# Weight words put together in PSUM banks, the root's scratch in a bank, and the value product on 128 rows, in an attention and mixture kernel

## The chip, the cores and the metric

The kernel runs on one core of a Trainium2 chip. The time is the device time of the whole program in microseconds (us); runs are compared by their median. A core has five engines that work side by side, each through its own list of instructions in a fixed order: TensorE (PE in the profile; its weight loads are PEld), VectorE (DVE), ScalarE (ACT), GpSimd (POOL) and SyncE (SP, which here only issues transfers). SBUF is the working memory. PSUM has eight banks of 128 rows by 512 four-byte words; TensorE writes its products there, and VectorE and ScalarE read and write it in this kernel.

## The reference

Attention over 8 batches, 12 heads, 448 positions and head width 64, with the queries and keys normalised by their root mean square, and behind it a channel-mixing layer of width 768 with 1024 hidden units. Weights come as 8-byte floats.

```python
def rmsnorm(x, g):
    rms = np.sqrt(np.mean(x * x, axis=-1, keepdims=True) + 1e-06)
    return x / rms * g
q_n, k_n = (rmsnorm(q, g_q), rmsnorm(k, g_k))
scores = 1.0 / np.sqrt(64) * np.matmul(q_n, k_n.transpose(0, 1, 3, 2))
attn = softmax(scores)                       # exp(scores - max) / (sum + 1e-09)
x = matmul(attn, v), heads side by side      # (8, 448, 768)

x_prev = x moved down by one position, zeros first
xk = mu_k * x + (1.0 - mu_k) * x_prev
xr = mu_r * x + (1.0 - mu_r) * x_prev
k = np.maximum(xk @ w_k, 0.0)
v = k * k @ w_v
r = 1.0 / (1.0 + np.exp(-(xr @ w_r)))
return r * v
```

## The kernel before, in words

Products run on 16-bit halves: each operand is split into a high part and a low part ("hi", "lo"), and three of the four products are summed in a bank.

Three streams of work are written out and interleaved. A small planner in the kernel's last loop always lets the stream with the smallest clock write its next piece (rates such as `ATT_STEPS` and `W_RATE2`); behind it a scheduler orders each engine's instructions by its own model of their times. The order that the chip runs is fixed by that, and it is shown below for the places that matter.

*Attention.* The 48 pairs of heads go one after the other; two pairs make a quad. `load` fetches keys and queries of a quad. `prep` normalises them: ScalarE squares (L166), GpSimd folds the squares (L167) and multiplies the keys with the gains (L169), VectorE sums (L170), scales (L172, L173) and takes the reciprocal root in `rsqrt` (L67 to L72, a guess from the bits and three Newton rounds, on 128x28 numbers); GpSimd multiplies by it (L179), ScalarE takes the high part (L184), GpSimd the low part (L186, "nat"), and transfers on SyncE's queue turn them into the stacks "stk". `vprep` finds a power of two to scale each pair's values: ScalarE squares and sums (L203), a tiny matmul spreads the sums (L204) into the bank "tr", VectorE takes the maximum (L206), and the values are split (L211, L215). `group_scores` multiplies for two tiles of 128 rows at a time (the last group has one) into a bank for each tile, VectorE takes the maximum (L258), ScalarE the exponential (L259). `group_probs` scales by the sum (L271, L272) into high (ScalarE, L277) and low (VectorE, L278), and a transfer transposes them to "pT". `attend` makes the value product in the bank "av": eleven passes for each head, of which the one on the low part of slot 3 uses 64 rows and the others 128; ScalarE reads it out (L303).

*Weights.* `weight_tile` builds 20 tiles of 128 columns: eight of w_k, six of w_r, six of w_v. Each is loaded in two chunks of 384 (w_k, w_r) or 512 (w_v) numbers a row, so 28 and 12 chunks. The two halves of an 8-byte float are put together to a 4-byte one: ScalarE scales the upper half's magnitude (L403), VectorE shifts (L404), ors in bits of the lower half (L405) and the sign (L406). Then a Gram product in "av" (L412), its diagonal (L416), a sum over rows (L417) and a maximum (L418) give the tile's scale, and the tile is split into 16-bit halves (on GpSimd and ScalarE for tiles 1 to 13, L423 to L425, else L427 and L428).

*The mixing layer.* `moe` takes each batch when its six pairs are done: `mix` (L367 to L376), then `prod` (L456) with the key weights (xk, wk), the gate weights (xr, wr) and the output weights (kk, wv), each into one of two banks "mm".

The eight banks before: "sc" four and "mm" two, "av" one, "tr" one. In the first six pairs (`PRO`) every third score tile lies in an "mm" bank.

```python
tag, nb = ("mm", MM_BUFS) if i < PRO and (i * NT + t0 + j) % 3 == 2 else ("sc", 4)
banks.append(ps.tile([P, 512], F32, name=tag, bufs=nb))
```

Of the kernel before, what the change touches and what calls it, by code (L numbers as in the profile page):

```python
# [7 lines left out]
F32 = mybir.dt.float32  # L8
F16 = mybir.dt.float16
BF16 = mybir.dt.bfloat16  # L10
I32 = mybir.dt.int32
AF = mybir.ActivationFunctionType
ALU = mybir.AluOpType
# [15 lines left out]
PRO = 6  # L29
# [34 lines left out]
def rsqrt(nc, pool, y, a, n, tag):  # L64
    t = pool.tile([P, n], F32, name=tag)
    yi = y.bitcast(I32)
    nc.vector.tensor_scalar(out=yi, in0=a.bitcast(I32), scalar1=1, scalar2=None, op0=ALU.logical_shift_right)  # L67
    nc.vector.tensor_scalar(out=yi, in0=yi, scalar1=-1.0, scalar2=float(0x5F3759DF), op0=ALU.mult, op1=ALU.add)
    for _ in range(NEWTON):
        nc.vector.tensor_tensor(out=t, in0=y, in1=y, op=ALU.mult)  # L70
        nc.vector.scalar_tensor_tensor(out=t, in0=t, scalar=-0.5, in1=a, op0=ALU.mult, op1=ALU.mult)
        nc.vector.scalar_tensor_tensor(out=y, in0=t, scalar=1.5, in1=y, op0=ALU.add, op1=ALU.mult)  # L72


def attn_moe_kernel(tc, q, k, v, g_q, g_k, mu_k, mu_r, w_k, w_v, w_r, out):
# [14 lines left out]

    def allmax(src, n, r):
        pt = ps.tile([P, 512], F32, name="tr", bufs=1)
# [21 lines left out]
    rsqrt(nc, small, gm[:, 1:2], gm[:, 0:1], 1, "rs1")  # L114
# [46 lines left out]
    def prep(u):  # L161
        ss = small.tile([P, 2 * NSS], F32, name="ss", bufs=2)
# [11 lines left out]
        rsqrt(nc, small, ss[:, NSS:2 * NSS], ss[:, 0:NSS], NSS, "rs28")  # L174
        yield
        T = [ap_.tile([P, 2, 2 * NT, HD], F16, name="stk", bufs=3) for x in range(2)]
        for n, t in enumerate(LD.pop(u)):
            tv = t.rearrange("p h (t d) -> p (h t) d", d=HD)
            nc.gpsimd.tensor_tensor(out=tv, in0=tv, in1=spread(ss[:, NSS + 2 * NT * n:NSS + 2 * NT * (n + 1)], HD), op=ALU.mult)  # L179
# [13 lines left out]
    def vprep(i):  # L193
# [8 lines left out]
        pt = ps.tile([P, 512], F32, name="tr", bufs=1)  # L202
# [34 lines left out]
    def group_scores(i, t0, n):  # L237
# [5 lines left out]
        for j in range(n):  # L243
            tag, nb = ("mm", MM_BUFS) if i < PRO and (i * NT + t0 + j) % 3 == 2 else ("sc", 4)
            banks.append(ps.tile([P, 512], F32, name=tag, bufs=nb))
# [41 lines left out]
    PASSES = [(hl, c, P) for c in range(3) for hl in range(2)] + [(0, 3, P), (1, 3, HD)] + [(0, c, P) for c in range(4, 7)]  # L287
# [104 lines left out]
    def weight_tile(nm, w, kt, c, ci):  # L392
# [4 lines left out]
        for i in range(0, kt, hk):  # L397
# [5 lines left out]
            nc.scalar.activation(out=f[:, i:i + hk, :], in_=top.bitcast(F32), func=AF.Abs, scale=F64_EXP)  # L403
            nc.vector.tensor_scalar(out=fb, in0=fb, scalar1=3, scalar2=None, op0=ALU.logical_shift_left)  # L404
            nc.vector.scalar_tensor_tensor(out=fb, in0=low, scalar=29, in1=fb, op0=ALU.logical_shift_right, op1=ALU.bitwise_or)  # L405
# [204 lines left out]
```

## Time and profile before

| what | value |
|---|---|
| median of 3 runs | 1267.06 us (1266.27 to 1267.16) |
| profiled execution | 1263.01 us |
| its span, first to last instruction | 1261.2 us |
| mean granted TensorE clock | 0.911 |
| TensorE busy | 1017.4 us (81%) |
| VectorE busy | 901.4 us (71%) |
| ScalarE busy | 794.4 us (63%) |
| GpSimd busy | 681.4 us (54%) |

Busy time is the sum over a whole run of stages that differ. In rows of groups, "L405 DVE ... wf<-raw,wf 128x384 ... x28 | 23.1, 835 | 0.1" reads: line 405, VectorE, writes tile wf from raw and wf, 28 instructions, 23.1 us in all, 835 ns each, and 0.1 us of idle time of that engine just before them. In rows of single lines three durations stand as minimum/median/maximum. In rows of waits stand the total, the number of times and the longest, in us. The rows of stages give for each engine its busy us in the stretch, then the granted TensorE clock, the DMA engines' busy share and GB/s.

### The profile page before, as it was taken

Reading aid. Unit: us, or ns where it says so; the run is one execution under the profiler, and the core shown is the slowest. Engines: PE = TensorE matmul, PEld = TensorE weight load, DVE = VectorE, ACT = ScalarE, POOL = GpSimd, SP = SyncE. Lnnn points to the kernel's source line nnn. Section 1 sums busy time; section 2 is a strip of 40 time slices with the busy share of each in tenths; the row PEclk is TensorE's granted clock in tenths of the full one; section 3 lists DMA queues with packets and bytes.
Section 4 is the critical chain, followed back from the end, with each engine's and each line's share of the span. In section 5 each row is a group of like instructions: output and inputs, shape, how many; then the busy total and the mean of one; then the engine's idle time right before and its main releaser. Section 6 shows DMA issues by size and latency. Waiting matters only on the chain. (4 is left out here: it accounts for less than half of the span.)

```text
span 1261.2 us, 18897 instructions
## 1 busy us (share of the span) xinstructions
PE 1017.4 (81%) x5935; PEld 471.4 (37%) x5935; DVE 901.4 (71%) x2356; ACT 794.4 (63%) x1756; POOL 681.4 (54%) x678
## 2 busy tenths in 40 slices
PE   1125545586799999889999899898989999999998
PEld 0002222233244344433443444344434444344454
DVE  5886899979967868675786667776887687667200
ACT  3266656566756777577676765776778676876311
POOL 2642465736655657375467536674568455523731
PEclk9956656588799999998999999999989999999999
DMA  7589977978586878768777676978986787776101
GB/s 161 119 152 168 178 155 160 172 153 165 110 148 134 146 145 167 139 131 142 143 147 147 128 138 138 167 132 152 167 162 129 151 150 125 136 144 102 26 13 38
DMA packets 456356, 172.77 MB, mean 137 GB/s; under 512 B 411200, under 2 KB 452672, under 8 KB 456256
## 3 DMA queue, kind: packets, MB, share of 16 engines
q1 hardware_dynamic: 423328, 132.24, 59.2%
q10 hardware_dynamic: 32928, 39.34, 12.8%
q8 instruction: 46, 0.75, 0.2%
q14 instruction: 54, 0.44, 0.1%
HBM read 61.41 MB, written 11.01 MB: 57 GB/s over the span
## 5 line engine op out<-in xcount | busy, mean ns | idle before, releaser
L278 DVE SCALAR_TENSOR_TENSOR ph<-sc,sums,ph 128x448 f16<-128x448 f32 x322 | 210.0, 676 | 87.8 <-ACT ph L277 87.2
L259 ACT ACTIVATE sc<-sc,sums 128x448 f32<-128x448 f32 x322 | 193.3, 612 | 108.8 <-DVE sums L258 91.5
L235 PE MATMUL sc<-stk 64*128 64x448 f16 (+1 forms) x1104 | 189.9, 379 | 68.1 <-DVE ph L278 49.7
L456 PE MATMUL mm<-wvh,kk 128*128 128x384 f16 x896 | 234.6, 330 | 0.1
L456 PE MATMUL mm<-xk,wkh 128*128 128x448 f16 x768 | 220.9, 366 | 12.7 <-ACT kf L478 6.0
L277 ACT ACTIVATE ph<-sc,sums 128x448 f16<-128x448 f32 x322 | 189.6, 645 | 50.3 <-DMA pT<-ph 15.7
L258 DVE TENSOR_REDUCE sums<-sc 128x1 f32<-128x448 f32 x322 | 187.8, 613 | 22.8 <-PE sc L235 22.3
L456 PE MATMUL mm<-wrh,xr 128*128 128x384 f16 x672 | 178.4, 329 | 6.9 <-ACT th L512 4.7
L235 PE MATMUL av<-pT,vh 128*64 128x448 f16 x672 | 142.0, 389 | 40.8 <-DMA pT<-ph 26.0
L456 PEld LDWEIGHTS <-kk 128*128 128x128 f16 x1344 | 125.8, 98 | 101.0 <-issue 25.3
L456 PE MATMUL mm<-wvl,kk 128*128 128x384 f16 x448 | 147.5, 329 | 0.0
L456 PE MATMUL mm<-xk,wkl 128*128 128x448 f16 x384 | 140.6, 366 | 0.0
L186 POOL TENSOR_TENSOR nat<-qk,nat 128x896 f16<-128x896 f32 x48 | 91.2, 1900 | 74.4 <-ACT nat L184 74.3
L167 POOL TENSOR_TENSOR xs<-xs 128x448 f32<-128x448 f32 x48 | 56.2, 1172 | 138.1 <-ACT xs L166 138.0
L235 PEld LDWEIGHTS <-stk 64*128 64x128 f16 (+1 forms) x1152 | 57.6, 101 | 193.5 <-issue 142.3
L456 PEld LDWEIGHTS <-xr 128*128 128x128 f16 x1008 | 93.1, 98 | 85.1 <-issue 23.6
L373 DVE SCALAR_TENSOR_TENSOR df<-x,bsc,df 128x448 f32<-128x448 f32 x90 | 90.7, 1018 | 35.8 <-POOL df L372 35.6
L179 POOL TENSOR_TENSOR qk<-qk,ss 128x896 f32<-128x896 f32 x48 | 82.0, 1728 | 60.2 <-DVE ss L72 49.2
L456 PE MATMUL mm<-wrl,xr 128*128 128x384 f16 x336 | 110.5, 329 | 0.0
L456 PEld LDWEIGHTS <-wkh 128*128 128x128 f16 x768 | 72.8, 100 | 92.8 <-issue 39.0
L516 POOL TENSOR_TENSOR o<-th,bsc 128x384 f32<-128x384 f32 x48 | 43.2, 899 | 104.8 <-DVE th L515 68.1
L166 ACT ACTIVATE xs<-qk 128x896 f32<-128x896 f32 x48 | 45.8, 954 | 79.3 <-DMA qk<-in_q_dram 50.8
(124 smaller groups left out, 1722.2 us busy)
## 6 DMA issues: line engine op xcount, KB each, us to landing
vf<-in_v_dram SPq DMA_DIRECT2D x48, 224.0 KB, 3.8
qk<-in_k_dram ACTq DMA_DIRECT2D x48, 224.0 KB, 4.9
qk<-in_q_dram ACTq DMA_DIRECT2D x48, 224.0 KB, 4.8
out_dram<-o SPq DMA_DIRECT2D x56, 192.0 KB, 2.9
vf<-in_v_dram SPq DMA_DIRECT2D x48, 192.0 KB, 3.8
raw<-in_moe_w_k_dram ACTq DMA_DIRECT2D x16, 384.0 KB, 3.9
raw<-in_moe_w_v_dram ACTq DMA_DIRECT2D x12, 512.0 KB, 4.7
raw<-in_moe_w_r_dram ACTq DMA_DIRECT2D x12, 384.0 KB, 4.5
```

The costliest lines, as they stand in the source:

```text
L166: nc.scalar.activation(out=xs, in_=tv, func=AF.Square)
L167: nc.gpsimd.tensor_tensor(out=xs[:, :, 0:HD // 2], in0=xs[:, :, 0:HD // 2], in1=xs[:, :, HD // 2:], op=ALU.add)
L179: nc.gpsimd.tensor_tensor(out=tv, in0=tv, in1=spread(ss[:, NSS + 2 * NT * n:NSS + 2 * NT * (n + 1)], HD), op=ALU.mult)
L186: nc.gpsimd.tensor_tensor(out=lo, in0=t4, in1=hi, op=ALU.subtract)
L235: return op(**kw)
L258: nc.vector.tensor_reduce(out=sums[:, t:t + 1], in_=sp[:, 0:S], axis=AX.X, op=ALU.max, negate=True)
L259: nc.scalar.activation(out=sp[:, 0:S], in_=sp[:, 0:S], func=AF.Exp, bias=sums[:, t:t + 1], accum_out=sp[:, S:S + 1])
L277: nc.scalar.activation(out=ph[:, j, 0:S], in_=sp[:, 0:S], func=AF.Copy, scale=r[:, j:j + 1])
L278: nc.vector.scalar_tensor_tensor(out=ph[:, j, S:], in0=sp[:, 0:S], scalar=r[:, j:j + 1], in1=ph[:, j, 0:S], op0=ALU.mult, op1=ALU.subtract)
L373: nc.vector.scalar_tensor_tensor(out=df, in0=xc, scalar=sc[:, MX + j:MX + j + 1], in1=df, op0=ALU.mult, op1=ALU.add)
L456: nc.tensor.matmul(out=ps_, lhsT=la(i, a), rhs=ra(i, c), start=(i == 0 and a + c == 0), stop=(i == n - 1 and a == 1))
L516: nc.gpsimd.tensor_tensor(out=o[:, hs].rearrange("p (c n) -> p c n", n=P), in0=th.rearrange("p (c n) -> p c n", n=P), in1=spread(rsu[:, ND ...
```

## The change

Four things change.

- `weight_tile`: the first three of the four steps that put a word together work in a bank of the "mm" ring (ScalarE writes it, VectorE shifts in it and ors into it); the last or reads the bank and writes the tile wf in SBUF. Before, all four worked in wf. The steps are now L407 to L410.
- `rsqrt` and `prep`: the sums, the first guess and the scratch of the root lie in a new bank "misc" that is held for the whole program, with two halves for alternate quads; only the result y lies in SBUF. The Newton step is written so that each instruction has one input in the bank and one in SBUF. The number of instructions is the same, but for one copy at the start. They are now L65 to L70.
- The bank "tr" is gone: `vprep`'s tiny product (and two at the start) use "av". Score tiles of the first six pairs no longer use "mm", only the four "sc" banks.
- `attend`: the pass on the low part of slot 3 uses 128 rows.

```diff
-PRO = 6
...
-def rsqrt(nc, pool, y, a, n, tag):
-    t = pool.tile([P, n], F32, name=tag)
-    yi = y.bitcast(I32)
-    nc.vector.tensor_scalar(out=yi, in0=a.bitcast(I32), scalar1=1, scalar2=None, op0=ALU.logical_shift_right)
-    nc.vector.tensor_scalar(out=yi, in0=yi, scalar1=-1.0, scalar2=float(0x5F3759DF), op0=ALU.mult, op1=ALU.add)
+def rsqrt(nc, y, a, t):
+    ti = t.bitcast(I32)
+    nc.vector.tensor_scalar(out=ti, in0=a.bitcast(I32), scalar1=1, scalar2=None, op0=ALU.logical_shift_right)
+    nc.vector.tensor_scalar(out=y.bitcast(I32), in0=ti, scalar1=-1.0, scalar2=float(0x5F3759DF), op0=ALU.mult, op1=ALU.add)
     for _ in range(NEWTON):
-        nc.vector.tensor_tensor(out=t, in0=y, in1=y, op=ALU.mult)
-        nc.vector.scalar_tensor_tensor(out=t, in0=t, scalar=-0.5, in1=a, op0=ALU.mult, op1=ALU.mult)
+        nc.vector.tensor_tensor(out=t, in0=a, in1=y, op=ALU.mult)
+        nc.vector.scalar_tensor_tensor(out=t, in0=t, scalar=-0.5, in1=y, op0=ALU.mult, op1=ALU.mult)
         nc.vector.scalar_tensor_tensor(out=y, in0=t, scalar=1.5, in1=y, op0=ALU.add, op1=ALU.mult)
...
+    misc = ps.tile([P, 512], F32, name="misc", bufs=1)
+
     def allmax(src, n, r):
-        pt = ps.tile([P, 512], F32, name="tr", bufs=1)
+        pt = ps.tile([P, 512], F32, name="av", bufs=1)
...
-    rsqrt(nc, small, gm[:, 1:2], gm[:, 0:1], 1, "rs1")
+    nc.vector.tensor_copy(out=misc[:, 510:511], in_=gm[:, 0:1])
+    rsqrt(nc, gm[:, 1:2], misc[:, 510:511], misc[:, 511:512])
...
     def prep(u):
-        ss = small.tile([P, 2 * NSS], F32, name="ss", bufs=2)
+        y = small.tile([P, NSS], F32, name="ss", bufs=2)
+        o = (u % 2) * 2 * NSS
+        ss, tm = misc[:, o:o + NSS], misc[:, o + NSS:o + 2 * NSS]
...
-        rsqrt(nc, small, ss[:, NSS:2 * NSS], ss[:, 0:NSS], NSS, "rs28")
+        rsqrt(nc, y, ss, tm)
...
-            nc.gpsimd.tensor_tensor(out=tv, in0=tv, in1=spread(ss[:, NSS + 2 * NT * n:NSS + 2 * NT * (n + 1)], HD), op=ALU.mult)
+            nc.gpsimd.tensor_tensor(out=tv, in0=tv, in1=spread(y[:, 2 * NT * n:2 * NT * (n + 1)], HD), op=ALU.mult)
...
-        pt = ps.tile([P, 512], F32, name="tr", bufs=1)
+        pt = ps.tile([P, 512], F32, name="av", bufs=1)
...
-            tag, nb = ("mm", MM_BUFS) if i < PRO and (i * NT + t0 + j) % 3 == 2 else ("sc", 4)
-            banks.append(ps.tile([P, 512], F32, name=tag, bufs=nb))
+            banks.append(ps.tile([P, 512], F32, name="sc", bufs=4))
...
-    PASSES = [(hl, c, P) for c in range(3) for hl in range(2)] + [(0, 3, P), (1, 3, HD)] + [(0, c, P) for c in range(4, 7)]
+    PASSES = [(hl, c, P) for c in range(3) for hl in range(2)] + [(0, 3, P), (1, 3, P)] + [(0, c, P) for c in range(4, 7)]
...
-            nc.scalar.activation(out=f[:, i:i + hk, :], in_=top.bitcast(F32), func=AF.Abs, scale=F64_EXP)
-            nc.vector.tensor_scalar(out=fb, in0=fb, scalar1=3, scalar2=None, op0=ALU.logical_shift_left)
-            nc.vector.scalar_tensor_tensor(out=fb, in0=low, scalar=29, in1=fb, op0=ALU.logical_shift_right, op1=ALU.bitwise_or)
-            nc.vector.scalar_tensor_tensor(out=fb, in0=top, scalar=-0x80000000, in1=fb, op0=ALU.bitwise_and, op1=ALU.bitwise_or)
+            z = ps.tile([P, 512], F32, name="mm", bufs=MM_BUFS)[:, 0:hk * P].rearrange("p (i n) -> p i n", n=P)
+            zi = z.bitcast(I32)
+            nc.scalar.activation(out=z, in_=top.bitcast(F32), func=AF.Abs, scale=F64_EXP)
+            nc.vector.tensor_scalar(out=zi, in0=zi, scalar1=3, scalar2=None, op0=ALU.logical_shift_left)
+            nc.vector.scalar_tensor_tensor(out=zi, in0=low, scalar=29, in1=zi, op0=ALU.logical_shift_right, op1=ALU.bitwise_or)
+            nc.vector.scalar_tensor_tensor(out=fb, in0=top, scalar=-0x80000000, in1=zi, op0=ALU.bitwise_and, op1=ALU.bitwise_or)
```

The scheduler orders all five engines anew. Three places, each before and now.

First, GpSimd's list near the start, from the fourth folding of squares or the first product with the root on. The tiles qk_129 and qk_132 before, qk_130 and qk_133 now, are the keys and queries of quad 0; those with qk0 and qk1 are quad 1's. Before:

```order
L167 TENSOR_TENSOR xs_298<-xs_298 128x14x32
L167 TENSOR_TENSOR xs_685<-xs_685 128x14x32
L169 TENSOR_TENSOR qk_625<-qk_625,gq_77 128x896
L179 TENSOR_TENSOR qk_129<-qk_129,ss_159 128x896
L179 TENSOR_TENSOR qk_132<-qk_132,ss_159 128x896
L423 TENSOR_SCALAR wf_255<-wf_255,WSC_112 128x768
L179 TENSOR_TENSOR qk0_139<-qk0_139,ss_264 128x896
L179 TENSOR_TENSOR qk1_142<-qk1_142,ss_264 128x896
L186 TENSOR_TENSOR nat_193<-qk_129,nat_193 128x2x7x64
```

Now:

```order
L182 TENSOR_TENSOR qk_130<-qk_130,ss_160 128x896
L182 TENSOR_TENSOR qk_133<-qk_133,ss_160 128x896
L170 TENSOR_TENSOR xs_302<-xs_302 128x14x32
L189 TENSOR_TENSOR nat_194<-qk_130,nat_194 128x2x7x64
L427 TENSOR_SCALAR wf_257<-wf_257,WSC_113 128x768
L189 TENSOR_TENSOR nat_207<-qk_133,nat_207 128x2x7x64
L170 TENSOR_TENSOR xs_696<-xs_696 128x14x32
L172 TENSOR_TENSOR qk_635<-qk_635,gq_78 128x896
```

Quad 0's products with the root and its subtraction now stand ahead of the work for quads 1 and 2, which stood between and in front of them.

Second, VectorE's list at the second pair's tiny product. WSC is a weight tile's maximum, read from "av"; vs is the tiny product's. Before:

```order
L418 TENSOR_REDUCE WSC<-av 128x1
L206 TENSOR_REDUCE vs<-tr 128x1
L172 TENSOR_SCALAR ss<-ss 128x14
L70 TENSOR_TENSOR rs_178<-ss 128x28
L419 TENSOR_SCALAR WSC<-WSC 128x1
```

Now:

```order
L422 TENSOR_REDUCE WSC<-av 128x1
L410 SCALAR_TENSOR_TENSOR wf<-raw,mm 128x384
L408 TENSOR_SCALAR mm<-mm 128x384
L423 TENSOR_SCALAR WSC<-WSC 128x1
L209 TENSOR_REDUCE vs<-av 128x1
L409 SCALAR_TENSOR_TENSOR mm<-raw,mm 128x384
```

Both maxima are now read from the one bank "av", so the tiny matmul on TensorE comes between the two reads, and other rows of VectorE with it.

Third, ScalarE's list among the last weight tiles and the first batch's products. kf reads a product out of "mm". Before:

```order
L478 ACTIVATE kf<-mm,RSC 128x448
L403 ACTIVATE wf<-raw 128x512
L399 DMA raw<-in_moe_w_v_dram 128x4x256
L479 ACTIVATE kk<-kf 128x448
L259 ACTIVATE sc<-sc,sums 128x448 x2
L403 ACTIVATE wf<-raw 128x512
```

Now:

```order
L482 ACTIVATE kf<-mm,RSC 128x448
L261 ACTIVATE sc<-sc,sums 128x448 x2
L187 CAST nat<-qk 128x2x7x64
L483 ACTIVATE kk<-kf 128x448
L407 ACTIVATE mm<-raw 128x512
L401 DMA raw<-in_moe_w_v_dram 128x4x256
L279 ACTIVATE ph<-sc,sums 128x448 x2
L150 DMA qk<-in_q_dram 64x2x448 x2
L482 ACTIVATE kf<-mm,RSC 128x448
```

The chunk's first step writes a bank that a product held just before, and the next product needs one of the same two.

## The prediction

> **What bounds the kernel now.** I read the page's busy slices first and then the stages by time, because one mean over the span would mix two regimes.
>
> ```profile
> span 1261.2 us, 18897 instructions
> DVE  5886899979967868675786667776887687667200
> ```
> ```profile
> core 0: us, PE busy (x) PEld busy (x) DVE busy (x) ACT busy (x) POOL busy (x), PEclk, DMA share, GB/s
> 0.00:94.00 94.00, 17.33 (x78) 7.39 (x78) 69.17 (x180) 38.44 (x70) 43.93 (x33) 0.85 0.69 145
> 94.00:317.00 223.00, 129.12 (x666) 55.55 (x667) 193.35 (x496) 140.77 (x292) 117.80 (x101) 0.66 0.85 163
> 317.00:402.00 85.00, 73.48 (x440) 34.24 (x438) 65.28 (x175) 54.97 (x126) 47.14 (x51) 0.91 0.73 134
> 402.00:1131.00 729.00, 674.52 (x4024) 308.22 (x4021) 534.56 (x1419) 515.05 (x1164) 424.74 (x439) 0.98 0.77 144
> ```
>
> The cuts at 94 and 317 us are the starts of the first and the ninth pair's value product; the weights are finished at about the second cut. VectorE's slices show 8 and 9 tenths in the first ten and then 6 to 8. In the first 317 us TensorE is busy 146 us and VectorE 69.17 + 193.35 = 262.5; between 94 and 317 VectorE is at 87% and no other engine over 63%. From 402 to 1131 it is the other way round: TensorE 93%, VectorE 73%. So VectorE sets the pace of the opening, and what the change does to VectorE counts there first. These are the groups that it touches, in the window from 0 to 317 us (count, then busy us and mean ns):
>
> ```profile
> L405 DVE SCALAR_TENSOR_TENSOR wf<-raw,wf 128x384 int32<-128x384 int32 x28 | 23.1, 835 | 0.1
> L406 DVE SCALAR_TENSOR_TENSOR wf<-raw,wf 128x384 int32<-128x384 int32 x28 | 21.7, 774 | 0.1
> L404 DVE TENSOR_SCALAR wf<-wf 128x384 int32<-128x384 int32 x28 | 21.2, 766 | 12.1 <-ACT wf L403 12.1
> L406 DVE SCALAR_TENSOR_TENSOR wf<-raw,wf 128x512 int32<-128x512 int32 x12 | 11.8, 984 | 0.0
> L405 DVE SCALAR_TENSOR_TENSOR wf<-raw,wf 128x512 int32<-128x512 int32 x12 | 11.2, 936 | 0.0
> L404 DVE TENSOR_SCALAR wf<-wf 128x512 int32<-128x512 int32 x12 | 8.6, 714 | 1.5 <-ACT wf L403 1.5
> L72 DVE SCALAR_TENSOR_TENSOR ss<-rs,ss 128x28 f32<-128x28 f32 x21 | 7.7, 369 | 0.1
> L71 DVE SCALAR_TENSOR_TENSOR rs<-rs,ss 128x28 f32<-128x28 f32 x21 | 6.3, 301 | 0.0
> L70 DVE TENSOR_TENSOR rs<-ss 128x28 f32<-128x28 f32 x21 | 5.4, 256 | 0.1
> L67 DVE TENSOR_SCALAR ss<-ss 128x28 int32<-128x28 int32 x7 | 5.2, 743 | 0.0
> L172 DVE TENSOR_SCALAR ss<-ss 128x14 f32<-128x14 f32 x8 | 4.9, 608 | 0.0
> L68 DVE TENSOR_SCALAR ss<-ss 128x28 int32<-128x28 int32 x7 | 3.6, 518 | 0.0
> ```
>
> A mean of 743 ns for 28 elements cannot be work. Two rows of the timeline (start us, us), and the spread of single lines (min/median/max ns), say what it is:
>
> ```profile
> 35.62 3.08 POOL L169 TENSOR_TENSOR qk<-qk,gq 128x896 f32<-128x896 f32 x1
> 36.66 2.07 DVE L67 TENSOR_SCALAR ss<-ss 128x28 int32<-128x28 int32 x1
> ```
> ```profile
> L404 DVE TENSOR_SCALAR wf<-wf x40: 334/410/1965, 19.1 to 302.2; 128x384 int32<-128x384 int32 x28, 128x512 int32<-128x512 int32 x12
> L72 DVE SCALAR_TENSOR_TENSOR ss<-rs,ss x72: 161/186/1828, 29.4 to 1050.7; 128x28 f32<-128x28 f32 x72
> ```
>
> L67 begins while GpSimd multiplies and ends at 38.73, just after that multiply's end at 38.70. Half of all L72 take under 186 ns and the longest 1828. So a VectorE instruction whose tensors all lie in SBUF can stand still until a GpSimd instruction is over; the means above are mostly such waits. [...]
>
> **The change, part by part.** After it, no step of the word-building or of the root reads two tensors from SBUF; one side is a PSUM bank. VectorE has instructions of that kind already:
>
> ```profile
> L515 DVE SCALAR_TENSOR_TENSOR th<-th,mm 128x384 f32<-128x384 f32 x56 | 30.6, 547 | 64.2 <-PE mm L456 63.9
> L258 DVE TENSOR_REDUCE sums<-sc 128x1 f32<-128x448 f32 x322 | 187.8, 613 | 22.8 <-PE sc L235 22.3
> L271 DVE TENSOR_SCALAR sums<-sc 128x1 f32<-128x1 f32 x322 | 47.2, 151 | 66.9 <-ACT sc L259 65.7
> L208 DVE TENSOR_SCALAR bstat<-vs 128x1 int32<-128x1 int32 x48 | 7.1, 148 | 0.6
> ```
>
> *Words.* The nearest row is L515: one input from a bank, one from SBUF, 384 elements, 547 ns. I take it for all three steps of a chunk of 384. From L515 to L258 an element costs (613 - 547)/64 = 1.03 ns, so 512 elements need 547 + 132 = 679. The first step pays for this: alone it took 334 ns in SBUF, now 547; but its mean was 766. A chunk of 384 saves 835 + 774 + 766 - 3 x 547 = 734 ns, 28 of them 20.6 us; a chunk of 512 saves 984 + 936 + 714 - 3 x 679 = 597 ns, 12 of them 7.2 us. Together 27.8 us. No VectorE row writes a long tensor into a bank; I bound such a step by 334 and 613, and at 613 it would be 40 x 3 x 0.066 = 8 us less. ScalarE's first step of a chunk, L403, keeps its length as far as I can price it, and ScalarE has room.
>
> *Root.* With L72's median of 186 ns for each step: 21 x (183 + 115 + 70) + 7 x (557 + 332) + 8 x 422 ns = 7.7 + 6.2 + 3.4 = 17.3 us in the opening. L271 against L208, 151 from a bank and 148 from SBUF, says that a bank costs a small instruction nothing.
>
> [...]
>
> So VectorE has 27.8 + 17.3 = 45 us less to do in the opening. How much of it moves the end? VectorE idles 317 - 262.5 = 54.5 us there; if that stayed, all 45 would be gained, and if every saved wait turned into another, nothing. Up to 94 us the gain shows in the first scores:
>
> ```profile
> 46.42 3.45 POOL L179 TENSOR_TENSOR qk<-qk,ss 128x896 f32<-128x896 f32 x2 [0.85 <-DVE ss L72]
> 49.83 4.21 POOL L186 TENSOR_TENSOR nat<-qk,nat 128x896 f16<-128x896 f32 x2
> 59.83 0.55 PE L235 MATMUL sc<-stk 64*128 64x448 f16 x2 [12.96 <-DMA stk<-nat]
> ```
>
> GpSimd's order now has quad 0's subtraction ahead of quad 1's two products (the first place shown with the change): 3.45 us less in front of it, and the root before that ends some 4 us sooner. So the scores start about 8 us earlier, and with shorter GpSimd waits I count 9. The other 30 of the 45 lie between 94 and 317. VectorE has 30 us of idle time there already, where it hands over to ScalarE between maximum, exponential and probabilities, and the DMA share is 0.85 of 223 us, 190 us of transfers that stay: so about half comes through, 16. Sum 25.
>
> *Banks.* A third of the first six pairs' score tiles lay in "mm" banks; now the four "sc" banks hold all, as they do for later pairs. The little product of the value scales (L204, L206) moves from its own bank to "av", which weight tiles and value products hold in turn.
>
> ```profile
> PE sc L235 <- DVE ph L278: 28.4, 7, 15.2
> PE mm L235 <- DVE ph L278: 16.4, 6, 6.1
> L206 DVE TENSOR_REDUCE vs<-tr x48: 205/215/226, 14.1 to 1140.4; 128x1 f32<-128x64 f32 x48
> ```
>
> These are TensorE's waits for score banks in the opening (us, times, longest). They cost little while VectorE is the bound; the price shows in L258's row: over the 42 later pairs with four banks VectorE waited 22.3 us for scores, half a us a pair, so 3 us for six. The little product waits on TensorE until the weight tile's last maximum is read; behind it stand the next tile's Gram matmuls or scores, and on VectorE behind its reader L206 the steps that give ScalarE the values' scale. The order puts two to five rows between the two reads (second place), 0.3 us at the least, which covers a hand-over but not the reader's own 0.22 and a second hand-over back: I take 0.4 us each time, ten times, 4 us.
>
> *Value product.* 96 matmuls take 128 rows in place of 64, at 402 ns for 397: nothing.
>
> ```profile
> L235 PE MATMUL av<-pT,vl 128*64 128x448 f16 x288 | 70.8, 402 | 0.0
> L235 PE MATMUL av<-pT,vl 64*64 64x448 f16 x96 | 19.6, 397 | 0.0
> POOL qk L179 <- DVE ss L72: 49.2, 12, 10.4
> ```
>
> *After 402.* The roots' waits go there too. VectorE has 27% to spare, so that covers most; but GpSimd waits 49.2 us in the run for the root's last step, and some of it delays stacks. I count 4, between 0 and 10.
>
> Sum: 25 + 4 - 3 - 4 = **22 us**. The profiled execution took 1263.0 us, its span 1261.2, and the median of the runs lies 4.1 above it. So a profile at 1241 and **a median of 1245 us**.
>
> **The rivals.**
>
> *All of it comes through.* Idle time stays at 54.5 us and the opening loses 45; the other terms give 2 on balance, 4 later less 2 for the banks: 1267 - 47 = 1220. For it: the idle pieces are short, and TensorE's clock of 0.66 in the second stage may rise as gaps close. Against: the DMA share, over 1 in part of that stage. Chance 0.17.
>
> ```profile
> 94.00:126.00 32.00, 16.81 (x91) 6.92 (x92) 22.00 (x76) 20.50 (x50) 9.53 (x9) 0.61 1.06 166
> ```
>
> *The opening has another bound close behind.* Transfers, or the ring of VectorE, ScalarE and TensorE over four score banks, keep the ninth value product near 310, so that 9 of the start less 7 for the banks is left: 1265, or down to 1258 where a few us of the rest come through. For it: 44.8 us of waits for score banks, and the transfers. Against: VectorE at 87%. Chance 0.19, of which 0.08 within 0.2%.
>
> *Slower, by the "mm" ring.* The last weight chunks and the eight products of the first L456 batch now take turns in two banks, and ScalarE's order has them alternating (third place).
>
> ```profile
> L403 ACT ACTIVATE wf<-raw 128x512 f32<-128x512 f32 x12 | 8.0, 670 | 9.3 <-DMA raw<-in_moe_w_v_dram 8.8 <-POOL x L305 0.5
> L456 PE MATMUL mm<-xk,wkh 128*128 128x448 f16 x96 | 32.1, 407 | 8.2 <-ACT kf L478 4.8 <-POOL xk L376 3.3
> ```
>
> If each product waits out one chunk's chain, 0.67 on ScalarE and 3 x 0.68 on VectorE, that is 8 x 2.7 = 22 us; and if a chunk's bank is still being read out by ScalarE, which I price like L403's 0.67, VectorE's queue waits at the word-building's first step, 12 x 0.67 = 8 us. Then 1245 + 30 = 1275; it decides from 22 us of such waits on. Against it: 18 matmuls at 0.41 are 7.4 us, longer than a chunk's chain, so one bank can be emptied under the other's product. Chance 0.09.
>
> *Banks cost each small step more than I take.* [...] Against it: L271 and L208. Chance 0.05.
>
> **How the numbers follow.** The forecast has 0.50 and, for itself, 1233 to 1256. About 0.2%, 2.5 us, is what a measurement of this kernel can tell from no change. Faster: 0.50 + 0.17 + 0.11 + 0.05 = 0.83; within 0.2% 0.08; slower 0.09. The range, 1220 to 1266, takes in the case that all comes through and the one that little does, and leaves the ring out.
>
> **What would show it.** Right: the word-building's steps near 547 and 679 ns with a maximum close to the mean, the root's near 186; L169 on GpSimd (3.08 above) shorter; first scores near 51 us, the ninth value product before 300. Wrong: steps over 613 ns; VectorE waiting for ScalarE before the word-building's first step for over 25 us (12.1 + 1.5 now); or the ninth value product still near 317 with VectorE under 80%, which would name another bound of the opening.

## The result, and the profile after

The changed kernel takes **1213.24 us** (median of runs from 1207.29 to 1216.88), the kernel before beside it 1266.66 us: ratio 0.959, 95% interval 0.9555 to 0.9625. Forecast were 1245 us and 1220 to 1266. The direction was right; the gain is 53 us where 22 were counted, and the time lies outside the range.

The profiled execution took 1216.9 us, its span 1215.1. Its stages, cut as before at the starts of the 1st, 9th, 13th and 46th value product (columns as in the prediction's table of stages):

```profile
span 1215.1 us, 18885 instructions
DVE  4577788887977577676877676857775578666200
```
```profile
0.00:84.00 84.00, 15.32 (x66) 6.17 (x67) 50.10 (x172) 35.84 (x63) 42.48 (x34) 1.00 0.84 162
84.00:291.00 207.00, 124.38 (x674) 59.66 (x675) 165.15 (x503) 142.59 (x296) 107.16 (x101) 0.71 0.88 173
291.00:379.00 88.00, 73.36 (x442) 35.31 (x443) 70.46 (x190) 60.79 (x138) 51.19 (x54) 0.93 0.81 146
379.00:1085.00 706.00, 660.48 (x4015) 308.16 (x4012) 505.52 (x1412) 511.48 (x1159) 423.79 (x435) 0.98 0.85 148
```

| stage ends at value product | before, us | after, us | gained | forecast |
|---|---|---|---|---|
| 1st | 94 | 84 | 10 | 9 |
| 9th | 223 | 207 | 16 | 16 |
| 13th | 85 | 88 | -3 | -7 (banks, all of the opening) |
| 46th | 729 | 706 | 23 | 4 |
| end | 130 | 130 | 0 | 0 |

Read by this table alone, three stages came out as forecast, and the step that failed is the one after 402 us. The experiments show that this reading is wrong: the first rows fit in part for another reason.

The groups of VectorE that the change touches, from 0 to 291 us (count, busy us, mean ns, idle before and its releaser). L408 to L410 are the former L404 to L406, L68 and L70 two of the root's former steps, L70 and L72:

```profile
L408 DVE TENSOR_SCALAR mm<-mm 128x384 int32<-128x384 int32 x28 | 15.6, 560 | 20.7 <-ACT mm L407 20.6
L409 DVE SCALAR_TENSOR_TENSOR mm<-raw,mm 128x384 int32<-128x384 int32 x28 | 15.3, 553 | 0.1
L410 DVE SCALAR_TENSOR_TENSOR wf<-raw,mm 128x384 int32<-128x384 int32 x28 | 14.9, 542 | 0.4 <-POOL wrl L429 0.3
L408 DVE TENSOR_SCALAR mm<-mm 128x512 int32<-128x512 int32 x12 | 8.3, 695 | 6.0 <-ACT mm L407 6.0
L410 DVE SCALAR_TENSOR_TENSOR wf<-raw,mm 128x512 int32<-128x512 int32 x12 | 8.1, 678 | 0.0
L68 DVE TENSOR_TENSOR misc<-misc,ss 128x28 f32<-128x28 f32 x21 | 3.9, 187 | 0.2
L70 DVE SCALAR_TENSOR_TENSOR ss<-misc,ss 128x28 f32<-128x28 f32 x21 | 3.7, 178 | 0.2
```

The waits are gone, and the prices are those of the forecast: 542 to 560 ns for 384 elements (547 taken), 678 to 695 for 512 (679), 178 and 187 for the root's steps (186). No step of the words lasts over 700 ns, where single ones took up to 2419 before. VectorE has 50.10 + 165.15 = 215.3 us of work in the opening where it had 262.5: 47 us less, 45 forecast. But it idles 291 - 215.3 = 75.7 us there, against 54.5 before. The lists of waits (us, times, longest) say for what; first the kernel before, then the change:

```profile
DVE wf L404 <- ACT wf L403: 13.5, 9, 5.7
ACT wf L403 <- DMA raw<-in_moe_w_k_dram: 12.5, 5, 4.8
```
```profile
DVE mm L408 <- ACT mm L407: 26.6, 20, 4.6
ACT mm L407 <- DMA raw<-in_moe_w_k_dram: 21.1, 12, 4.8
DVE sums L260 <- PE sc L238: 16.4, 5, 11.0
```

VectorE waits twice as long for ScalarE's first step of a chunk, and that step waits for the weights to land. It also waits 16.4 us for scores, 0.5 before.

### The profile page after: what moved, and what is told of

Same layout as the page of the kernel before. It is cut to its first block, busy times and chain, and to the rows that moved or that the text cites. A ratio compares the mean times of both kernels' runs of the same rounds, so it can differ in the third digit from the quotient of the medians.

```text
span 1215.1 us, 18885 instructions
## 1 busy us (share of the span) xinstructions
PE 996.6 (82%) x5935; PEld 476.4 (39%) x5935; DVE 828.9 (68%) x2357; ACT 794.8 (65%) x1756; POOL 672.3 (55%) x678
## 5 line engine op out<-in xcount | busy, mean ns | idle before, releaser
L261 ACT ACTIVATE sc<-sc,sums 128x448 f32<-128x448 f32 x336 | 201.6, 608 | 108.0 <-DVE sums L260 99.4
L280 DVE SCALAR_TENSOR_TENSOR ph<-sc,sums,ph 128x448 f16<-128x448 f32 x336 | 218.3, 677 | 68.4 <-ACT ph L279 66.1
L460 PE MATMUL mm<-xk,wkh 128*128 128x448 f16 x768 | 217.8, 363 | 11.6 <-ACT kf L482 10.1
L260 DVE TENSOR_REDUCE sums<-sc 128x1 f32<-128x448 f32 x336 | 196.3, 613 | 37.3 <-PE sc L238 36.7
L279 ACT ACTIVATE ph<-sc,sums 128x448 f16<-128x448 f32 x336 | 195.2, 642 | 31.9 <-DMA pT<-ph 10.1
L238 PE MATMUL av<-pT,vh 128*64 128x448 f16 x672 | 145.8, 387 | 63.4 <-DMA pT<-ph 49.9
L273 DVE TENSOR_SCALAR sums<-sc 128x1 f32<-128x1 f32 x336 | 49.6, 151 | 89.9 <-ACT sc L261 88.5
L238 PEld LDWEIGHTS <-vh 128*64 128x64 f16 x672 | 59.5, 117 | 113.7 <-issue 67.3
```

Of the source, the lines that this page charges most:

```text
L238: return op(**kw)
L260: nc.vector.tensor_reduce(out=sums[:, t:t + 1], in_=sp[:, 0:S], axis=AX.X, op=ALU.max, negate=True)
L261: nc.scalar.activation(out=sp[:, 0:S], in_=sp[:, 0:S], func=AF.Exp, bias=sums[:, t:t + 1], accum_out=sp[:, S:S + 1])
L273: nc.vector.tensor_scalar(out=r[:, j:j + 1], in0=sp[:, S:S + 1], scalar1=1e-9, scalar2=2.0 ** -15, op0=ALU.add, op1=ALU.mult)
L279: nc.scalar.activation(out=ph[:, j, 0:S], in_=sp[:, 0:S], func=AF.Copy, scale=r[:, j:j + 1])
L280: nc.vector.scalar_tensor_tensor(out=ph[:, j, S:], in0=sp[:, 0:S], scalar=r[:, j:j + 1], in1=ph[:, j, 0:S], op0=ALU.mult, op1=ALU.subtract)
```

## The experiments

A first theory, A, took the table at its word: VectorE's time sets the pace after 379 us as well, so the roots' shorter waits count there nearly one for one. The rivals: B, the instructions stand in another order, and the gain of the steady stage (13th to 46th value product) is that order's; C, the pass of the value product on 128 rows is quicker. All kernels below compute everything. The kernel before was timed anew beside each group of runs, at medians from 1262.6 to 1266.7 us; 1265 is their mean, and the ratios are to the runs of the same group. In the table, "first", "ninth" and "steady" are the start of the first and of the ninth value product and the length of the steady stage in the profiled execution, in us.

| kernel | median us | ratio to before, 95% | first | ninth | steady |
|---|---|---|---|---|---|
| before | 1265 | 1 | 94 | 317 | 729 |
| the change | 1213.2 | 0.959 (0.9555 to 0.9625) | 84 | 291 | 706 |
| v64 | 1215.5 | 0.9613 (0.956 to 0.9665) | 81 | 288 | 702 |
| root_sbuf | 1246.7 | 0.9847 (0.9808 to 0.9885) | 94 | 299 | 737 |
| words_sbuf | 1246.3 | 0.9838 (0.9794 to 0.9881) | 87 | 295 | 728 |
| both_sbuf | 1249.9 | 0.9878 (0.9832 to 0.9924) | 93 | 308 | 730 |
| both_att | 1252.6 | 0.9896 (0.9838 to 0.9953) | 92 | 307 | 724 |
| both_moe | 1248.4 | 0.988 (0.9814 to 0.9947) | 93 | 303 | 728 |
| n_att | 1228.8 | 0.9711 (0.9671 to 0.9752) | 84 | 299 | 725 |
| n_moe | 1224.8 | 0.9683 (0.9654 to 0.9711) | 84 | 292 | 715 |
| nb_att | 1246.7 | 0.9855 (0.9823 to 0.9887) | 95 | 314 | 713 |
| nb_moe | 1261.0 | 0.9988 (0.996 to 1.0015) | 94 | 317 | 729 |
| fix_root | 1233.6 | 0.9765 (0.9733 to 0.9798) | 84 | 296 | 716 |
| fix_words | 1220.9 | 0.9666 (0.9638 to 0.9695) | 87 | 295 | 702 |
| fix_both | 1239.2 | 0.9811 (0.9745 to 0.9876) | 88 | 302 | 713 |
| n_moe_root | 1239.4 | 0.9819 (0.9786 to 0.9852) | 86 | 296 | 723 |
| n_att_root | 1243.3 | 0.9848 (0.9804 to 0.9891) | 88 | 303 | 722 |
| b_first | 1239.9 | 0.9797 (0.9745 to 0.9849) | 86 | 296 | 721 |
| bf_att | 1238.4 | 0.981 (0.9782 to 0.9838) | 86 | 291 | 730 |
| bf_moe | 1239.1 | 0.981 (0.9775 to 0.9844) | 86 | 294 | 717 |

### The value product back on 64 rows

```diff
-    PASSES = ... [(0, 3, P), (1, 3, P)] ...
+    PASSES = ... [(0, 3, P), (1, 3, HD)] ...
```

> The changed kernel with the one pass of the value product back on 64 rows; every engine's order stays row for row that of the change. Theory A (after 379 us VectorE's time still sets the pace, so the roots' shorter waits count there too) and theory B (the steady stage gained from another order of the instructions): nothing moves, 1213 us within 3. Theory C (the 128-row pass makes the value products, and so the steady stage, quicker): the 23 us of the steady stage go back, 1236 us.

The same time within its interval, 1215.5 us, and with the same order on all engines a steady stage of 702 us. C falls. The two kernels also show how far two profiled executions of one order lie apart: 3 us in the first stage, 4 in the steady one.

### One part taken back, and the scheduler free to order anew

root_sbuf takes back the root's bank, words_sbuf the word-building's, both_sbuf both; in both_sbuf only the banks' new use and the 128-row pass are left of the change.

```diff
-    misc = ps.tile([P, 512], F32, name="misc", bufs=1)
+    misc = const.tile([P, 512], F32, name="misc")
```
```diff
-            z = ps.tile([P, 512], F32, name="mm", bufs=MM_BUFS)[:, 0:hk * P]...
-            (z, zi in the four steps)
+            (f[:, i:i + hk, :], fb in the four steps, as before)
```

> The changed kernel with the root's scratch in SBUF again (the words stay in PSUM). Theory A: VectorE has the roots' waits back, some 17 us in the opening and 29 us after it, of which about 10 and 23 count: 1213 + 33 = 1246 us, the steady stage between the 13th and the 46th value product back from 706 to about 729 us. Theory B: only the opening's 10 us come back, and the steady stage moves by what the new order happens to give: 1223 us with a scatter of some 10 either way. Theory C: 1223 us, steady stage 706.

> The changed kernel with the weights' words put together in SBUF again (the root stays in PSUM). Theories A and C: 27.8 us of VectorE's waits come back, all before the weights are done, and 16 of them count: 1229 us, with the steady stage still near 706 us. Theory B: the opening loses the same 16 us, and the steady stage, whose instructions are the change's own in another order, may move by 10 us or more from 706.

> The changed kernel with root and words both in SBUF again: only the banks' new use and the 128-row pass are left of the change. Theory A: all gains go, 1213 + 16 + 33 = 1262 us, about the kernel before. Theory C: the steady stage keeps its 23 us, 1239 us. Theory B: the opening's 26 us go, 1239 us, and the steady stage scatters with the order. If the banks' new use costs what the forecast gave it (7 us), 1269 us.

1246.7, 1246.3 and 1249.9 us. The first is A's number. The second is nobody's: without the words' bank the first two stages lose 4 us, not 16, and the steady stage, in which no word is built, goes from 706 to 728. The third is too fast for A (1262). Either part taken back loses 33 us, both together hardly more. Three things change in each of these kernels: the waits, the order, and sometimes the banks. They had to be taken apart.

### The same instructions in other orders

The scheduler orders by modelled times, so a pacing number that is off by one gives another order of thousands of rows and leaves every instruction as it is. n_att and n_moe are the changed kernel, nb_att and nb_moe the kernel before.

```diff
-ATT_STEPS = 126
+ATT_STEPS = 127
```
```diff
-MOE_STEPS = 93
+MOE_STEPS = 94
```

> The changed kernel with ATT_STEPS 127 for 126, a pacing number: the same instructions on the same tiles, and only the order in which the scheduler has them is another. Theory A: the gain is in the instructions, so 1213 us within 6. Theory B: the 23 us of the steady stage belong to the order found for the change, and another order loses a good part: 1225 to 1240 us.

> The changed kernel with MOE_STEPS 94 for 93, a second pacing number: again the same instructions in another order. Theory A: 1213 us within 6. Theory B: 1225 to 1240 us.

> The kernel before with ATT_STEPS 127 for 126: its own instructions in another order. Theory A: 1267 us within 6. Theory B: the order found for the kernel before was a poor one by chance, so another gains, 1245 to 1260 us; if orders scatter about evenly, some come out slower than 1267.

> The kernel before with MOE_STEPS 94 for 93: again its own instructions in another order. Theory A: 1267 us within 6. Theory B: 1245 to 1260 us, or a scatter of 10 us and more about 1267.

The order alone moves the changed kernel by 12 to 16 us and the kernel before by 4 to 19. The change was timed in the best of its three orders, and the kernel before in the worst of its three. The mean ratios are 0.967 (with v64 in the change's own order) against 0.995: in the mean of three orders each the change is worth 2.8%, 36 us, not 53. The steady stage of the changed kernel lies between 702 and 725 us, that of the kernel before between 713 and 729: most of the 23 us there belong to the order.

### The waits alone, at a fixed order

To bring back only the waits, the order was left as the scheduler had set it, and then the tile got another address: SBUF in place of a bank. Every instruction stands where it stood on its engine, with the same semaphores; the traces show the same order. The edit, shortened:

```diff
     with tile.TileContext(nc, schedule_with_timeline_sim=True) as tc:
         attn_moe_kernel(tc, *args)
+    end = locate(nc, gq)                 # 2 KB set aside in front of it
+    m = locate(nc, misc)                # the root's bank
+    m.type, m.addr, m.bank, m.base = end.type, end.addr - 2048, end.bank, end.base
```

fix_words does it with the 28 chunks of 384 (the 12 of 512 did not fit), fix_both with the chunks and the root (whose two sets of columns fall together to make room), n_moe_root and n_att_root with the root in the two other orders.

> The changed kernel, each instruction in the place that it has there on every engine; only after the order was set, the bank of the root's scratch was given an address in SBUF. So nothing but the waits comes back. Theory A (the roots' waits count nearly one for one after 379 us too): 10 us in the first stage and 23 in the steady one, 1214 + 33 = 1247 us. Theory B (the steady stage gained from its order): 10 us in the first stage alone, 1224 us, steady stage 706 us as in the change. Between the two, by the runs in five orders so far (steady stage 728 us on the mean with the root in SBUF, 715 with it in a bank): 13 us in the steady stage, 1237 us.

> The changed kernel, each instruction in its place; after the order was set, the 28 word-building chunks of 384 elements were given addresses in SBUF (the 12 of 512 stay in the banks). 20.6 of the words' 27.8 us of waits come back. Theory A as forecast (16 of the 30 us after the first value product count): 16 x 20.6/27.8 = 12 us more, 1226 us, all in the second stage (207 to 219 us). Theory D (about 205 us is another bound of that stage, since it took 205 us with the root in SBUF and 207 with the words in SBUF): 0 to 5 us more, 1214 to 1219 us. Both: the steady stage stays at 706 us within 4.

> The kernel with MOE_STEPS 94, each instruction in the place that it has there; only the root's scratch was given an address in SBUF after the order was set. Against 1224.8 us of that order with the root in a bank: theory A 1258 us, with 23 of the 33 in the steady stage (715 to 738); theory B 1235 us, steady stage 715; between the two 1248 us.

> The kernel with ATT_STEPS 127, each instruction in the place that it has there; only the root's scratch was given an address in SBUF after the order was set. Against 1228.8 us of that order with the root in a bank: theory A 1262 us, with 23 of the 33 in the steady stage (725 to 748); theory B 1239 us, steady stage 725; between the two 1252 us.

> The changed kernel, each instruction in its place; after the order was set, the root's scratch and the 28 word-building chunks of 384 elements got addresses in SBUF. Theory F (at one and the same order the waits are worth what the runs with one of them gave, and the rest of the gain is the order and the banks): 1214 + 19 + 7 = 1240 us, 25 less than the kernel before with nearly the same waits. Theory G (either part alone covers the opening, and only with both gone does the loss show): the second stage goes from 207 towards 223 us, 1250 us or more.

That the waits are back is seen in fix_words, from 0 to 295 us (L414 to L416 are the three steps):

```profile
L416 DVE SCALAR_TENSOR_TENSOR wf<-raw,mm 128x384 int32<-128x384 int32 x28 | 27.9, 1006 | 0.2 <-POOL wkl L435 0.2
L414 DVE TENSOR_SCALAR mm<-mm 128x384 int32<-128x384 int32 x28 | 22.0, 788 | 20.0 <-ACT mm L413 19.9
L415 DVE SCALAR_TENSOR_TENSOR mm<-raw,mm 128x384 int32<-128x384 int32 x28 | 20.3, 730 | 0.1
```

The same instructions take 788, 730 and 1006 ns where the change has 560, 553 and 542. For the root, the first step (from 0 to 296 us in fix_root, then in the change to 291):

```profile
L65 DVE TENSOR_SCALAR misc<-misc 128x28 int32<-128x28 int32 x7 | 5.7, 815 | 0.0
L65 DVE TENSOR_SCALAR misc<-misc 128x28 int32<-128x28 int32 x7 | 1.3, 183 | 0.0
```

By the ratios and 1265 us, the root's waits cost 21 us in the change's order (0.9765 against 0.960, the mean of the change and v64) and 17 in each of the others; the words' 8; both together 27, so within the error they add up. For the root that is between A (33) and B (10). Of the words A put 12 us into the second stage; there it is 1 (208 us against 207), and the opening is 4 us longer (7 against v64). Theory F's time is met, and G falls. The ratios' intervals make each of these uncertain by 4 to 8 us, and the waits of the 12 chunks of 512 are not among them.

Stages of fix_root:

```profile
0.00:84.00 84.00, 15.32 (x66) 6.28 (x67) 60.06 (x172) 35.85 (x63) 42.43 (x34) 1.00 0.78 161
84.00:296.00 212.00, 122.41 (x674) 58.86 (x675) 173.37 (x504) 142.85 (x296) 107.40 (x102) 0.71 0.87 169
386.00:1102.00 716.00, 660.90 (x4016) 308.24 (x4010) 520.77 (x1411) 510.99 (x1158) 423.54 (x435) 0.99 0.83 146
```

and of fix_both:

```profile
0.00:88.00 88.00, 15.28 (x65) 6.26 (x65) 65.53 (x169) 36.44 (x63) 45.30 (x34) 1.00 0.72 154
88.00:302.00 214.00, 122.37 (x674) 58.04 (x675) 183.54 (x506) 142.41 (x295) 110.27 (x101) 0.73 0.82 168
390.00:1103.00 713.00, 660.37 (x4017) 308.82 (x4016) 522.29 (x1414) 513.27 (x1164) 424.61 (x436) 0.99 0.83 146
```

In fix_root VectorE works 60 us in the first stage where the change has 50, and the first value product still starts at 84 (81 in v64): most of those 10 us of waits are hidden. In fix_both it works 65.53 + 183.54 = 249.1 us in the opening, 33.8 more than in the change, and the opening is 11 us longer; against v64, the same order as the change, it is 14. So a third to two fifths of the saved work move the end there, and the rest turns into idle time. In the steady stage 522.29 - 505.52 = 16.8 us of waits make it 7 us longer (713 against 706), 11 against v64. The stages come from one profiled execution each: 11 + 7 = 18 and 14 + 11 = 25 us stand beside the 27 of the ratios.

### One line of GpSimd's order, without the change

The change's order has one visible difference at the start. On GpSimd, quad 0's two products stand ahead of quad 1's second squares' sum and of quad 2's first sum and gains, and quad 0's low parts ahead of quad 1's products; before, it is the other way round. All kernels that the scheduler ordered with the root in a bank have it (the change, n_att, n_moe, words_sbuf). Of those with the root in SBUF none has quad 0's products first, and only root_sbuf has one of the two low parts ahead of the second pair of products. b_first forces it on the kernel before: quad 1's second squares' sum is queued behind quad 0's second product. Nothing else of the program is touched, but the scheduler then orders all the rest anew, so one such run could be a lucky order. bf_att and bf_moe do the same in two other orders.

```diff
+            with tc.issue_after(FIRST[-1].ins) if u == 1 and n else nullcontext():
                 nc.gpsimd.tensor_tensor(out=xs[:, :, 0:HD // 2], ...)       # prep, L167
...
-            nc.gpsimd.tensor_tensor(out=tv, in0=tv, in1=spread(...), op=ALU.mult)
+            p = nc.gpsimd.tensor_tensor(out=tv, in0=tv, in1=spread(...), op=ALU.mult)
+            if u == 0:
+                FIRST.append(p)
```

> The kernel before with one line that queues quad 1's second squares' sum on GpSimd behind quad 0's two products, as the change's order has it; root and words stay in SBUF. Theory F1 (the first stage's 10 us are GpSimd's order, not VectorE's waits): the first value product at 84 to 87 us, as in the change, against 94; the scheduler then orders all the rest anew, so the end is about 1265 - 8 = 1257 us with 10 us of scatter. Theory F2 (they are the root's waits, as forecast): first value product at 92 us or later.

> The kernel before with the one queueing line on GpSimd and ATT_STEPS 127. If the line itself is worth the gain: the first two stages end near 296 to 302 us (before 314 to 317 in its three orders) and the whole takes 1230 to 1242 us, under the 1247 us of this pacing without the line. If 1240 us with the line was a lucky order: 1250 to 1265 us.

> The same with MOE_STEPS 94. If the line itself is worth the gain: the first two stages end near 296 to 302 us, the whole 1235 to 1248 us, under the 1261 us of this pacing without the line. If not: 1250 to 1265 us.

1239.9, 1238.4 and 1239.1 us: with the line alone the kernel before has half of the change's gain. The first value product starts at 86 us, as F1 had it; the end comes sooner than the 1257 us within 10 that went with it. Against the same pacings without it the line is worth, by the ratios, 26, 6 and 23 us, 18 in the mean. The openings agree better: with the line they end at 296, 291 and 294 us, without it at 317, 314 and 317, so 21 to 23 us sooner in each order. What varies is the steady stage (8 us shorter, 17 longer, 12 shorter). The timeline of the kernel before (start us, us, what; waits in brackets), on GpSimd, SyncE's queue and TensorE:

```profile
34.53 1.12 POOL L167 TENSOR_TENSOR xs<-xs 128x448 f32<-128x448 f32 x1 [3.37 <-ACT xs L166]
38.66 3.64 POOL L179 TENSOR_TENSOR qk<-qk,ss 128x896 f32<-128x896 f32 x2
44.33 1.24 POOL L423 TENSOR_SCALAR wf<-wf,WSC 128x768 f32<-128x768 f32 x1 [2.03 <-DVE rs L70]
52.12 8.15 SPq L188 DMA_TRANSPOSE stk<-nat  x4
93.71 0.55 PE L235 MATMUL av<-pT,vh 128*64 128x448 f16 x1 [3.55 <-issue]
```

and of b_first:

```profile
32.98 3.69 POOL L182 TENSOR_TENSOR qk<-qk,ss 128x896 f32<-128x896 f32 x2 [5.75 <-DVE ss L72]
37.83 2.19 POOL L191 TENSOR_TENSOR nat<-qk,nat 128x896 f16<-128x896 f32 x1
42.21 2.17 POOL L191 TENSOR_TENSOR nat<-qk,nat 128x896 f16<-128x896 f32 x1
49.46 1.67 PE L240 MATMUL sc<-stk 64*128 64x448 f16 x7 [2.93 <-DMA stk<-nat]
86.11 0.55 PE L240 MATMUL av<-pT,vh 128*64 128x448 f16 x1 [3.63 <-DMA pT<-ph]
```

Before, GpSimd waits 3.37 us for quad 2's squares and multiplies by the gains (the prediction's row at 35.62) ahead of quad 0's products at 38.66; the weights' row at 44.33 waits another 2.03, then come quad 1's products, and only at 49.83 (the prediction's row) quad 0's low parts, whose transfers are issued from 52.12 us on. In b_first the products begin at 32.98 and the low parts at 37.83. The first scores start 10 us sooner, the first value product 8. The stages of b_first:

```profile
0.00:86.00 86.00, 15.89 (x71) 6.76 (x71) 70.17 (x178) 36.46 (x68) 41.26 (x32) 1.00 0.72 156
86.00:296.00 210.00, 121.01 (x675) 54.82 (x676) 188.06 (x501) 141.94 (x291) 119.74 (x100) 0.72 0.93 177
```

Here VectorE has all its waits, 70.17 + 188.06 = 258.2 us of work against 262.5, and the opening ends at 296 us in place of 317. Its idle time fell from 54.5 to 37.8 us, and the DMA share of the second stage rose from 0.85 to 0.93. With scores at hand by 50 us VectorE has more to do: in the stretch from 50 to 100 us it is busy 43.6 us, before 37.6, and the two other orders agree (43.7 each with the line, 37.2 and 37.3 without). From 50 to 150 us its waits for the first step of a chunk fall from 7.2 to 0.9 us and those for ScalarE's high parts of the probabilities (ph) from 11.5 to 3.4; its waits for the exponentials rise from 5.3 to 7.3. First b_first, then the kernel before:

```profile
50.00:100.00 50.00, 19.51 (x104) 6.87 (x99) 43.64 (x114) 28.46 (x64) 24.67 (x18) 0.99 0.86 157
```
```profile
50.00:100.00 50.00, 16.31 (x83) 5.52 (x83) 37.58 (x88) 24.97 (x56) 23.91 (x14) 0.69 0.86 155
```

### The banks' new use

both_att and both_moe are both_sbuf with the two pacing numbers.

> The changed kernel with root and words in SBUF and ATT_STEPS 127: what is left of the change is the banks' new use, in a second order (1249.9 us in the first). If the new use of the banks is worth something by itself, 1245 to 1252 us, under the kernel before in the mean of its orders (1258 us); if it is worth nothing, around 1258 us; if it costs the 7 us of the forecast, 1265 us.

> The same with MOE_STEPS 94, a third order. The same three answers: 1245 to 1252 us, 1258 us, or 1265 us.

1252.6 and 1248.4 us: mean ratio of the three orders 0.9885, of the kernel before 0.9948. The second stage takes 215, 214 and 211 us against 223, 220 and 223 before. The banks' new use costs nothing that these runs show. It seems to be worth some 8 us, but that is less than the scatter of the kernel before over its own orders.

## Why the prediction was wrong, step by step

**The prices of the work: right.** 47 us less for VectorE in the opening, 45 forecast; the words' steps lie within 3% of their price, the steps of the root that are shown within 5%. That a step with one side in a bank does not stand still for GpSimd was the author's estimate; as far as these runs go it held: no step of the words lasts over 700 ns in the change, and moving the operand alone took the last one from 542 to 1006 ns (fix_words).

**"So VectorE sets the pace of the opening": the step that failed.** The 87% left 30 us of idle time in that stage, and the step let the opening's length follow VectorE's work. b_first and its two companions show that this is not so: nearly the same VectorE work (258 us against 262) and an opening 21 to 23 us shorter in three orders. VectorE is busier there, 90% of the second stage, since quad 0's stacks, held up before in GpSimd's queue, give it work sooner. That these stacks are what matters among all that the scheduler moved with the line is read from the timelines and was not tried by itself. From this step came the next two errors.

**"About half comes through, 16", and "up to 94 us ... 9".** The numbers were met in part by another cause, which is luck. At one order 33.8 us of waits moved the opening by 11 to 14, of which 7 lie in the second stage (fix_both 214, the change and v64 207) and 4 to 7 in the first. The rest goes with the new order, whose visible part is the early place of quad 0. It was in the prediction, and priced at "3.45 us less in front of it": the one instruction moved, without the waits that this instruction brought along, and for the first scores alone. Its effect on the whole second stage, 13 us in b_first, had no term in the sum.

The first scores make this plainer. They were to start near 51 us and start at 57.90:

```profile
41.10 3.20 SPq L191 DMA_TRANSPOSE stk<-nat  x2
45.41 5.29 SPq L191 DMA_TRANSPOSE stk<-nat  x2
57.90 2.42 PE L238 MATMUL sc<-stk 64*128 64x448 f16 x12 [17.98 <-DMA stk<-nat]
83.90 0.58 PE L238 MATMUL av<-pT,vh 128*64 128x448 f16 x1 [5.76 <-DMA pT<-ph]
```

The stacks' transfers are issued 11 us sooner than before (41.10 against 52.12) but the first scores start only 2 us sooner. In v64, the same order, they start at 55.0 us, in b_first at 49.5. One could think that faster words fetch the next weights sooner and so crowd the stacks' transfers; the runs do not bear it out. In the change's order and with the words in the banks fix_root starts at 53.1, with slower words fix_both starts at 54.7 and fix_words at 55.6. What holds the transfers up stays open. From the first scores to the first value product the change and v64 take 26 us, fix_both 33, the kernel before 34. So the saved VectorE time is seen there, and the early start is seen only in part.

**"After 402: 4, between 0 and 10": about right for the waits, wrong for the stage.** With the order fixed the steady stage is 7 us shorter without the waits (11 against v64); for the root alone 10 in the change's order, 8 and -3 in the two others. What came on top, of 23, goes with the order: the same instructions took 702 to 725 us there in three orders.

**Banks, -7: wrong in sign or zero.** TensorE's waits for score banks in the opening, 28.4 + 16.4 us before, are these in the change (us, times, longest):

```profile
PE sc L238 <- DVE ph L280: 24.3, 10, 6.0
```

and three orders with the banks' new use alone are no slower than the kernel before. **Value product, 0: right** (v64).

**The sum.** The waits were forecast at 25 + 4 = 29 us, the early scores included, and measured at 27 at one order, without the chunks of 512. What the sum lacked is a term for the order: about half of the 53 us. The halves meet: fix_both (the change's order with the waits) and b_first (the kernel before with the line) both take 1239 to 1240 us. Part of the order's half is a gain that every kernel ordered with the root in a bank got here, the early place of quad 0; the rest is which of several orders each kernel happened to have, up to 19 us for the same instructions. How these two divide is not settled to better than the scatter of three orders each, and the parts overlap: line (18 in the mean), waits (27) and banks (8) add to more than the 36 us that the change is worth over orders.

**The rivals.** "All of it comes through" gave 1220 us, near the measured time, for a cause that is refuted: VectorE's idle time did not stay, it rose to 75.7 us. "Another bound close behind" had part of the mechanism, since VectorE came to wait longer for weights and for scores, and not the outcome: the ninth value product starts at 291 us and not near 310. Of the "mm" ring one sign came true: VectorE waits 20.6 + 6.0 = 26.6 us for ScalarE before L408, over the 25 that were to show the forecast wrong. The ring is not the reason. By the lists of waits ScalarE waits 33.9 us for weights ahead of that step (23.4 before) and for no bank, and TensorE's products wait 1.1 us for a bank that a chunk held. Of the rival that banks cost each small step more, with its 0.05 among the faster outcomes, no run shows the dearer step: means of 178 and 187 ns in a bank (L70 and L68 of the change) against a median of 186 in SBUF (L72 before).

## What to carry to other kernels

When a change makes a scheduler order thousands of rows anew, a measured gain is waits plus order; give the order a term and a width in the forecast (here up to 19 us for identical instructions), and part the two by moving the operand after the order is set or by timing each kernel in several orders. A busy share near 90% does not by itself make an engine's work the bound (87% here, and the stage got 13 us shorter with nearly the same work): ask what its work is waiting for, and look along the other queues at the program's start. Here one line that took instructions of later blocks out of the way of the first block's last steps shortened the opening by 21 to 23 us, and the whole by 6 to 26, against 27 for all the waits at a fixed order.

## What was unexpected of the hardware

In the rows above the column of the granted TensorE clock cannot be taken at its word in the first 100 us. From 50 to 100 us it gives 0.69 for the kernel before and 0.99 for b_first, at 16.31 and 19.51 us of TensorE time. The score products are equally long in both (minimum/median/maximum ns), from 48 to 74 us before and in b_first, and then from 500 to 600 us before:

```profile
L235 PE MATMUL sc<-stk x12: 507/574/578, 59.8 to 62.8; 64*128 64x448 f16 x12
L240 PE MATMUL sc<-stk x18: 527/574/577, 49.5 to 69.9; 64*128 64x448 f16 x12, 64*64 64x448 f16 x6
L235 PE MATMUL sc<-stk x96: 346/349/373, 505.5 to 596.1; 64*128 64x448 f16 x72, 64*64 64x448 f16 x24
```

In the traces the first entry of the clock stands 63.1 us (before) and 92.4 us (b_first) after the start, and the column counts the time ahead of it as full clock (1.00 from 0 to 50 us in both). So the higher clock in b_first's rows is no cause of its shorter first stage. In the second stage the column gives 0.72 against 0.66; whether that adds to the gain was not tried.
